# A fused attention, Fourier and MLP kernel on one core: weights fetched a step before they are converted, conversions tied to a place on VectorE, and a batch's products without padding

## Chip, cores and metric

One core of a Trainium2 chip runs the whole program as one launch. The metric is the device time of an execution in microseconds, and the median over the runs stands for the kernel. TensorE is called PE, VectorE DVE, ScalarE ACT, GpSimd POOL, and SyncE, which issues most DMAs, SP.

## The reference

Three layers follow one another. B=2, H=8, S=768, D=48, so the model width is 384. `w_ch1` and `w_ch2`, `w_in` and `w_out` arrive as float64, `w_sg` as float32.

```python
def _attn_ref(r, k, v, w, u):
    for t in range(S):
        kt, vt, rt, wt = (k[:, :, t], v[:, :, t], r[:, :, t], w[:, :, t])
        cur = np.einsum('bhd,bhe->bhde', u[None] * kt, vt)
        y[:, :, t] = np.einsum('bhd,bhde->bhe', rt, state + cur)
        state = wt[:, :, :, None] * state + np.einsum('bhd,bhe->bhde', kt, vt)

def _moe_ref(x, w_ch1, w_ch2):
    mixed = np.real(np.fft.fft(np.fft.fft(x, axis=1), axis=2)).astype(np.float32)
    u = x + mixed
    un = (u - mean(u)) / np.sqrt(var(u) + 1e-06)
    return u + np.maximum(un @ w_ch1, 0.0) @ w_ch2

def _moe2_ref(x, w_in, g_ln, w_sg, b_sg, w_out):
    u, v = split(gelu(x @ w_in))
    v_n = (v - mean(v)) / np.sqrt(var(v) + 1e-06) * g_ln
    v_s = np.einsum('ts,bsd->btd', w_sg, v_n) + b_sg[None, :, None]
    return x + (u * v_s) @ w_out
```

## The kernel before

**Attention.** Eight pairs of heads, n = 0 to 7; batch 0 has n = 0 to 3, batch 1 the others. A pair's 768 tokens are six chunks of 128. `prep` (L185) loads decays, r, k and v and scales them on DVE. `own_term` (L266) makes the term of u: six products dg_ps of the elementwise r·k with two columns of u, then dv on DVE. `scores` (L289) makes the products sc_ps of r and k in a chunk and masks them on DVE. `chunk_states` (L304) turns k with the identity (kn_ps), multiplies it with v (kv_ps) and runs the state through the chunks with a scan on DVE (U, L321). `values` (L326) adds what the state gives (L333) and what the chunk itself gives (L336) in y_ps. `radix6` (L340) starts the Fourier transform. Products in float32 take two instructions on PE. The products dg_ps, kn_ps, kv_ps and those of L336 are written 128 columns wide, though 2, 112, 96 and 96 of the columns are used; what lies past them is overwritten by the next product or not read.

**Fourier and MLP.** `fourier` (L404) transposes, runs the radix-3 step on DVE (L427 to L430, tiles t, sc and Z) and multiplies with tables (x_ps, gh). `moe1` (L508 on) works on four halves, n = 0 to 3, of 384 tokens, and for each through 12 blocks f of w_ch1 and w_ch2: z_ps, then z_hi on ACT and z_lo on DVE (L557), then ch. Values are kept as a rounded part (hi) and a rest (lo), and a product is three: hi·hi, hi·lo, lo·hi. `gating` multiplies with w_in (win), mixes over the tokens (s_ps, wsg) and multiplies with w_out (wout).

**Weights.** `narrow` (L155) fetches a piece of float64 with a DMA on SP into a raw tile and makes float32 of its words with three operations on DVE: L162, L163 and L164. The first two write the tile st, of which there are two. `weights(f)` (L823) does this for w1 and w2 of a block; ACT then copies hi (L837) and writes its negative (L838), and an accumulating DMA on POOL adds the raw value (L842, or L840 for two blocks). Blocks 1 and 3 use the tiles us_hi and us_lo as raw space, blocks 0, 2, 10 and 11 share one tile w_raw, the others use places of later blocks' weights. So a fetch waits for the accumulating DMA of the block that had the space before. `load_split` and `load_all` (L167, L179) do the same for win (8 pieces), wsg (12, without conversion) and wout (4), with two raw tiles.

**What sets the order.** The Python code emits the work of attention, Fourier, MLP and weights by turns: `merge` draws steps of two generators, and `ahead(n)` (L876) emits `weights(f)` for all blocks below n, one from the ninth step of the attention on (WA, WB), the first four before the MLP, later LA = 6 blocks ahead of the MLP's step. A scheduler then puts the instructions of each engine in a queue by its own estimates; each engine runs its queue in order, and an instruction that waits holds up what stands behind it. `after` (L151) ties later fetches to the last y of attention so far.

```python
        nc.vector.tensor_scalar(out=st, in0=top, scalar1=3, scalar2=0x3FFFFFF8, op0=ALU.logical_shift_left, op1=ALU.bitwise_and)
        nc.vector.scalar_tensor_tensor(out=st, in0=top, scalar=0xC0000000, in1=st, op0=ALU.bitwise_and, op1=ALU.bitwise_or)
        nc.vector.scalar_tensor_tensor(out=x, in0=low, scalar=29, in1=st, op0=ALU.logical_shift_right, op1=ALU.bitwise_or)
```

## Time and profile before

| | us |
|---|---|
| Median of three runs | 450.96 (449.62 to 455.56) |
| Profiled execution, its own time | 449.04 |
| Its span, first to last instruction | 447.3 |
| PE busy | 419.6 |
| DVE busy | 271.7 |
| ACT busy | 160.2 |
| POOL busy | 100.3 |

Times in the rows below count from the span's start. In an order of time, a row is start, duration in us, engine, line, operation, the tile written and those read, shape and count; what stands in brackets is how long the engine stood still before it, and what ended that. PE's mean granted clock over the span was 0.966 of full speed.

### The profile page before, as it was taken

The numbers are of one execution on the slowest core, as the hardware profiler recorded it, in microseconds if no ns is written. First come the engines' busy times: TensorE is split into PE (matmuls) and PEld (weight loads), VectorE is DVE, ScalarE is ACT, GpSimd is POOL, SyncE is SP. The second block draws the span as 40 slices with busy tenths as digits, with TensorE's granted clock in tenths as the row PEclk, the third lists the DMA queues.
The fourth block names the chain that finished last, engine by engine and source line by source line (L and its number), as shares of the span: only waits on it lengthen the run. The fifth ranks groups of instructions, "written<-read, shape, count | busy, mean of one in ns | idle before, by whom it ended". The sixth has DMA issues, their size and how long they took to land.

```text
span 447.3 us, 6662 instructions
## 1 busy us (share of the span) xinstructions
PE 419.6 (94%) x2502; PEld 398.2 (89%) x2502; DVE 271.7 (61%) x543; ACT 160.2 (36%) x365; POOL 100.3 (22%) x127
## 2 busy tenths in 40 slices
PE   9879959999899997999978999999989999999994
PEld 8769958897699996999968999999889998999994
DVE  5996869988589686656676316311488437502322
ACT  3432513732547265434234215313554214131100
POOL 2001210022313241311242002003455424001230
PEclk9657997999999999999999999999999999999998
DMA  7956793231276762203330000002432000200002
GB/s 247 318 131 164 233 271 77 36 116 27 98 264 113 190 106 74 34 1 91 120 90 18 2 0 1 0 1 70 125 88 72 0 3 1 88 19 0 1 21 95
DMA packets 17642, 38.09 MB, mean 85 GB/s; under 512 B 2304, under 2 KB 9344, under 8 KB 17472
## 3 DMA queue, kind: packets, MB, share of 16 engines
q1 hardware_dynamic: 14160, 31.66, 22.7%
q0 software_dynamic: 3440, 5.90, 7.3%
q8 instruction: 22, 0.36, 0.3%
q14 instruction: 20, 0.16, 0.1%
HBM read 28.70 MB, written 2.36 MB: 69 GB/s over the span
## 4 chain that ended last, share of the span: by engine, by line
PE 52%; DVE 16%; DMA 14%; issue 9%; ACT 4%; POOL 3%; SPq 1%; POOLq 0%; DVEq 0%; ACTq 0%
PE s_ps L112 11%; PE o_ps L112 6%; PE z_ps L112 6%; PE ch L112 5%; PE u_ps L112 5%; PE x_ps L115 4%; DMA w_raw<-in_w 3%; DMA us_hi<-in_w 3%; PE y_ps L336 3%; PE v_ps L112 3%; PE gh L115 2%; DMA raw<-in_win 2%; DMA raw<-in_wsg 2%; DMA w<-w_raw 2%; PE sc_ps L297 2%
## 5 line engine op out<-in xcount | busy, mean ns | idle before, releaser
L112 PE MATMUL z_ps<-us_hi,w 128*128 128x384 f32 x288 | 79.3, 340 | 2.6 <-ACT us_hi L532 2.1
L112 PE MATMUL ch<-z_hi,w 128*128 128x384 f32 x288 | 80.4, 339 | 0.5 <-ACT z_hi L556 0.5
L557 DVE SCALAR_TENSOR_TENSOR z_lo<-z_ps,z_hi 128x384 fp32r<-128x384 f32 x48 | 26.6, 553 | 60.5 <-ACT z_hi L556 60.5
L112 PEld LDWEIGHTS z_ps<-us_hi,w 128*128 128x128 f32 x288 | 52.5, 188 | 4.1 <-ACT us_hi L532 2.7
L112 PEld LDWEIGHTS ch<-z_hi,w 128*128 128x128 f32 x288 | 52.3, 188 | 1.8 <-ACT z_hi L556 1.1
L112 PE MATMUL ch<-z_lo,w 128*128 128x384 f32 x144 | 49.4, 343 | 3.4 <-DVE z_lo L557 3.2
L112 PE MATMUL z_ps<-us_lo,w 128*128 128x384 f32 x144 | 48.4, 336 | 0.0
L556 ACT ACTIVATE z_hi<-z_ps 128x384 fp32r<-128x384 f32 x48 | 23.5, 490 | 57.7 <-PE z_ps L112 38.5
L642 DVE SCALAR_TENSOR_TENSOR t_g<-s_ps,g,bsg 128x384 f32<-128x384 f32 x16 | 9.5, 615 | 41.8 <-PE s_ps L112 41.8
L112 PE MATMUL s_ps<-wsg_hi,vn_hi 128*128 128x384 f32 x96 | 32.5, 339 | 0.0
L112 PE MATMUL s_ps<-wsg_lo,vn_hi 128*128 128x384 f32 x96 | 32.5, 339 | 0.0
L112 PE MATMUL s_ps<-wsg_hi,vn_lo 128*128 128x384 f32 x96 | 32.5, 339 | 0.0
L112 PEld LDWEIGHTS ch<-z_lo,w 128*128 128x128 f32 x144 | 27.0, 188 | 5.2 <-DVE z_lo L557 5.2
L646 POOL TENSOR_TENSOR vn_lo<-t_g,vn_hi 128x384 fp32r<-128x384 f32 x16 | 16.4, 1033 | 55.7 <-ACT vn_hi L645 55.7
L112 PEld LDWEIGHTS z_ps<-us_lo,w 128*128 128x128 f32 x144 | 27.1, 188 | 0.1
L842 POOL DMA_DIRECT2D w<-w_raw x10 | 12.2, 1220 | 64.9 <-DVE Xh L254 31.6
L336 PE MATMUL y_ps<-v,sc 128*128 128x128 f32 x144 | 24.7, 294 | 0.0
L336 PEld LDWEIGHTS y_ps<-v,sc 128*128 128x128 f32 x144 | 23.3, 213 | 0.1
L645 ACT CAST vn_hi<-t_g 128x384 fp32r<-128x384 f32 x16 | 8.0, 513 | 37.9 <-DVE t_g L643 27.9
L177 POOL TENSOR_TENSOR wsg_lo<-raw,wsg_hi 128x384 fp32r<-128x384 f32 x12 | 12.4, 1036 | 32.3 <-ACT wsg_hi L176 32.2
L115 PE MATMUL x_ps<-dft,Z 128*128 128x256 f32 x72 | 16.9, 380 | 2.7 <-DVE Z L430 2.7
L509 POOL TENSOR_TENSOR z_lo<-uc,z_hi 128x384 fp32r<-128x384 f32 x7 | 7.1, 1010 | 50.4 <-ACT z_hi L508 50.4
(232 smaller groups left out, 963.7 us busy)
## 6 DMA issues: line engine op xcount, KB each, us to landing
w_raw<-in_w SPq DMA_DIRECT2D x20, 384.0 KB, 5.3
w<-w_raw POOLq DMA_DIRECT2D x10, 384.0 KB, 4.5
rk<-in_rk SPq DMA_DIRECT2D x4, 768.0 KB, 6.3
raw<-in_win SPq DMA_DIRECT2D x8, 384.0 KB, 3.3
v<-in_v SPq DMA_DIRECT2D x6, 384.0 KB, 5.9
raw<-in_wsg SPq DMA_DIRECT2D x12, 192.0 KB, 2.4
out<-o SPq DMA_DIRECT2D x12, 192.0 KB, 2.0
P<-in_wx SPq DMA_DIRECT2D x4, 387.0 KB, 4.8
```

The source lines that it names most:

```text
L112: nc.tensor.matmul(o, lhsT=x, rhs=y, start=start and i == 0, stop=stop and i == len(ps) - 1)
L115: nc.tensor.matmul(o, lhsT=a, rhs=b, start=start, stop=stop)
L177: nc.gpsimd.tensor_tensor(out=w.lo[:, to], in0=x, in1=w.hi[:, to].bitcast(F32), op=ALU.subtract)
L297: nc.tensor.matmul(sc_pss[h][:, i, :], lhsT=kt[hs, c * C:(c + 1) * C], rhs=rt[hs, c, :], start=True, stop=True)
L336: nc.tensor.matmul(y_ps[:, at:at + C], lhsT=sc[h][:, i, :], rhs=v[:, c], start=c == h == 0, stop=True, skip_group_check=True)
L509: nc.gpsimd.tensor_tensor(out=parts.lo, in0=x, in1=parts.hi.bitcast(F32), op=ALU.subtract)
L556: nc.scalar.activation(out=z.hi, in_=z_ps, func=AF.Relu)
L557: nc.vector.scalar_tensor_tensor(out=z.lo, in0=z_ps, scalar=0.0, in1=z.hi.bitcast(F32), op0=ALU.max, op1=ALU.subtract)
L642: nc.vector.scalar_tensor_tensor(out=t, in0=s_ps[h], scalar=g[:, f:f + 1], in1=bsg[:, hs], op0=ALU.mult, op1=ALU.add)
L645: nc.scalar.copy(vn.hi[:, f, 3 * h:3 * h + 3], th)
L646: nc.gpsimd.tensor_tensor(out=vn.lo[:, f, 3 * h:3 * h + 3], in0=th, in1=vn.hi[:, f, 3 * h:3 * h + 3].bitcast(F32), op=ALU.subtract)
L842: nc.gpsimd.dma_start(out=t[:, 1].bitcast(F32), in_=raw.bitcast(F32)[:, :, :NST], accum_op=ALU.add)
```

## The change

`narrow` is split: `fetch` issues the DMA and `narrow` only converts. `weights(f)` now only fetches and returns its tiles; `convert` does the rest, and `ahead` calls it for a block once the next one has been fetched (LAG = 1; LA goes from 6 to 7). `load_all` fetches piece o + 1 before it converts piece o. The first operation of every conversion is tied with `keep_in_program_order`: the scheduler may not put it ahead of the DVE operation that the program emitted just before it. In batch 1 dg_ps, kn_ps, kv_ps and the products of L336 are written 2, 112, 96 and 96 columns wide; batch 0 keeps 128.

```diff
@@ -26,7 +26,8 @@
 WA = 8
 WB = 3
 KC = 9
-LA = 6
+LA = 7
+LAG = 1
 RG = [[3,3,3,3],[0,0,0,0]]
 KV = range(8)
 NJ = 0
@@ -152,33 +153,44 @@
         if gate is not None:
             tc.add_manual_dep(getattr(ins, "ins", ins), getattr(gate, "ins", gate).name, mybir.DependencyInfo(mybir.DependencyClass.Sync, mybir.DependencyReason.DATA), reason="later weights")
 
-    def narrow(raw, src, o):
-
+    def fetch(raw, src, o):
         after(nc.sync.dma_start(out=raw, in_=src[:, o:o + NST]))
+
+    def narrow(raw):
         st = stage.tile([C, NST], U32, name="st", tag="st", bufs=2)
         word = raw.bitcast(U32).rearrange("p (n two) -> p n two", two=2)
         low, top = word[:, :, 0], word[:, :, 1]
         x = raw.bitcast(U32)[:, :NST]
-        nc.vector.tensor_scalar(out=st, in0=top, scalar1=3, scalar2=0x3FFFFFF8, op0=ALU.logical_shift_left, op1=ALU.bitwise_and)
+        first = nc.vector.tensor_scalar(out=st, in0=top, scalar1=3, scalar2=0x3FFFFFF8, op0=ALU.logical_shift_left, op1=ALU.bitwise_and)
+        if True:
+            tc.keep_in_program_order(first)
         nc.vector.scalar_tensor_tensor(out=st, in0=top, scalar=0xC0000000, in1=st, op0=ALU.bitwise_and, op1=ALU.bitwise_or)
         nc.vector.scalar_tensor_tensor(out=x, in0=low, scalar=29, in1=st, op0=ALU.logical_shift_right, op1=ALU.bitwise_or)
         return x.bitcast(F32)
 
-    def load_split(w, src, o, at):
-
-        to = slice(at, at + NST)
+    def load_piece(src, o):
+
         raw = raws[0].tile([C, NST], I64, name="raw", tag="raw", bufs=2)
         if src.dtype == I64:
-            x = narrow(raw, src, o)
-        else:
-            x = raw.bitcast(F32)[:, :NST]
-            nc.sync.dma_start(out=x, in_=src[:, o:o + NST])
+            fetch(raw, src, o)
+            return o, raw, None
+        x = raw.bitcast(F32)[:, :NST]
+        nc.sync.dma_start(out=x, in_=src[:, o:o + NST])
+        return o, raw, x
+
+    def split_piece(w, o, raw, x):
+        to = slice(o, o + NST)
+        if x is None:
+            x = narrow(raw)
         nc.scalar.copy(w.hi[:, to], x)
         nc.gpsimd.tensor_tensor(out=w.lo[:, to], in0=x, in1=w.hi[:, to].bitcast(F32), op=ALU.subtract)
 
     def load_all(w, src, n):
+        got = load_piece(src, 0)
         for o in range(0, n, NST):
-            load_split(w, src, o, o)
+            later_on = load_piece(src, o + NST) if o + NST < n else None
+            split_piece(w, *got)
+            got = later_on
             yield
 
 
@@ -277,7 +289,8 @@
         dg_ps = ps(b, [C, 512], "dg_ps", DB)
         for c in range(NC_):
 
-            nc.tensor.matmul(dg_ps[:, 2 * c:2 * c + C], lhsT=prod[:PR, c], rhs=uh[:, None, 2 * p:2 * p + 2].to_broadcast([PR, C // 2, 2]), start=True, stop=True)
+            k = C // 2 if b == 0 else 1
+            nc.tensor.matmul(dg_ps[:, 2 * c:2 * c + 2 * k], lhsT=prod[:PR, c], rhs=uh[:, None, 2 * p:2 * p + 2].to_broadcast([PR, k, 2]), start=True, stop=True)
         nc.vector.tensor_tensor(out=dv.rearrange("p c (h e) -> p c h e", h=2), in0=v[:, :, :2 * D].rearrange("p c (h e) -> p c h e", h=2),
                                 in1=dg_ps[:, :2 * NC_].rearrange("p (c h o) -> p c h o", h=2, o=1).to_broadcast([C, NC_, 2, D]), op=ALU.mult)
         return dv
@@ -304,15 +317,17 @@
     def chunk_states(ap, b, ends, kt, v, U):
 
         kn = ap([C, NC_ - 1, PR], "kn")
+        w = C if b == 0 else PR
         for g0, g1 in ((0, 3), (3, 5)):
             kn_ps = ps(b, [C, 3, C], "kn_ps", KB)
             for c in range(g0, g1):
-                nc.tensor.matmul(kn_ps[:, c - g0], lhsT=kt[:, c * C:(c + 1) * C], rhs=ident[:PR], start=True, stop=True)
+                nc.tensor.matmul(kn_ps[:, c - g0, :w], lhsT=kt[:, c * C:(c + 1) * C], rhs=ident[:PR, :w], start=True, stop=True)
             nc.scalar.copy(kn[:, g0:g1], kn_ps[:, 0:g1 - g0, :PR])
         kv_all = ps(b, [PR, 512], "kv_ps", VB)
         kv_ps = kv_all[:, :(NC_ - 1) * 2 * D].rearrange("p (c e) -> p c e", c=NC_ - 1)
         for c in range(NC_ - 1):
-            nc.tensor.matmul(kv_all[:, c * 2 * D:c * 2 * D + C], lhsT=kn[:, c], rhs=v[:, c], start=c == 0, stop=True, skip_group_check=c > 0)
+            e = C if b == 0 else 2 * D
+            nc.tensor.matmul(kv_all[:, c * 2 * D:c * 2 * D + e], lhsT=kn[:, c], rhs=v[:, c, :e], start=c == 0, stop=True, skip_group_check=c > 0)
         kvs = f_room([PR, 2 * D, NC_ - 1], "kvs") if b == 0 else ap([PR, 2 * D, NC_ - 1], "kn")
         for c in range(NC_ - 1):
             nc.scalar.activation(out=kvs[:, :, c], in_=kv_ps[:, c], func=AF.Copy, scale=ends[:PR, c:c + 1])
@@ -333,7 +348,8 @@
                 nc.tensor.matmul(y3[:, i, 0:3:2], lhsT=rt[:, c, :], rhs=U[:, :, c - 1], start=i == 0, stop=True, skip_group_check=True)
             for h in range(2):
                 at = (3 * i + h) * D
-                nc.tensor.matmul(y_ps[:, at:at + C], lhsT=sc[h][:, i, :], rhs=v[:, c], start=c == h == 0, stop=True, skip_group_check=True)
+                e = C if b == 0 else 2 * D
+                nc.tensor.matmul(y_ps[:, at:at + e], lhsT=sc[h][:, i, :], rhs=v[:, c, :e], start=c == h == 0, stop=True, skip_group_check=True)
         return nc.vector.tensor_tensor(out=yo.rearrange("p i (h e) -> p i h e", h=2), in0=y3[:, :, 0:3:2], in1=dv[:, c0:c0 + 3].rearrange("p i (h e) -> p i h e", h=2), op=ALU.add)
 
     def radix6(x, y, Z, es, G):
@@ -763,7 +779,7 @@
                 for i in range(2):
                     weight_pool(i, inner)
                 for f in range(NF1):
-                    weights(f)
+                    convert(*weights(f))
                 m1 = inner.enter_context(tc.tile_pool(name="m1", bufs=1))
                 run(moe1(m1, HALVES, uT, w1, w2))
             with tc.tile_pool(name="x2p", bufs=1) as pool:
@@ -831,8 +847,14 @@
         else:
             raw = wpool[0].tile([C, 2, NST], I64, name="w_raw", tag="w_raw")
         t = wpool[f >= NW].tile([C, 2, 2, DM], F32R, name=f"w_{f}", tag=f"w_{f}")
-        for i, (w, nm) in enumerate(((w1, "w1"), (w2, "w2"))):
-            x = narrow(raw[:, i] if raw is not None else us[i], ins[nm], f * DM)
+        places = us if raw is None else (raw[:, 0], raw[:, 1])
+        for place, nm in zip(places, ("w1", "w2")):
+            fetch(place, ins[nm], f * DM)
+        return f, t, raw, places
+
+    def convert(f, t, raw, places):
+        for i, w in enumerate((w1, w2)):
+            x = narrow(places[i])
             w[f] = Split(t[:, 0, i], t[:, 1, i])
             nc.scalar.copy(t[:, 0, i], x)
             nc.scalar.mul(t[:, 1, i], t[:, 0, i].bitcast(F32), -1.0)
@@ -871,13 +893,17 @@
                            a_room([C, 6 * DM], "Z").rearrange("p (z e) -> p z e", z=6))
             return made[b]
 
-        done = 0
-
-        def ahead(n):
+        done, fetched = 0, []
+
+        def ahead(n, most):
             nonlocal done
-            for f in range(done, min(n, NF1)):
-                weights(f)
-            done = max(done, min(n, NF1))
+            while done < min(n, most):
+                fetched.append(weights(done))
+                done += 1
+                while fetched and fetched[0][0] < done - LAG:
+                    convert(*fetched.pop(0))
+            while fetched and fetched[0][0] < n - LAG:
+                convert(*fetched.pop(0))
 
         m1 = low.enter_context(tc.tile_pool(name="m1", bufs=1, side="right"))
         early[0] = m1
@@ -891,7 +917,7 @@
                 if got == 0:
                     break
                 if n >= WA:
-                    ahead(min(GF, 1 + (n - WA) // WB))
+                    ahead(1 + (n - WA) // WB, GF)
             dump("y0", made[0][0])
             four = fourier(0, f_room, *made[0], uT[0])
             merge(islice(four, 4), att_steps, F0, False, LEAD)
@@ -914,10 +940,10 @@
                     dump("u0", uT[0])
                     late.close()
                     weight_pool(1, late, side="right")
-                ahead(min(12 * n + k + 1 + LA, NF1 if n or k >= E0 else NW))
+                ahead(12 * n + k + 1 + LA, NF1 if n or k >= E0 else NW)
                 yield
 
-        ahead(GF)
+        ahead(GF + LAG, GF)
         mixing = moe1(m1, HALVES, uT, w1, w2)
         merge(first(), second(), FR)
         att.close()
```

Three places in DVE's queue. The first is pair 3 of the attention: U_102 is its state scan, y_693 and prod belong to the next pair's `prep`, ab and Z to `radix6` of the pair before. Before:

```order
L347 TENSOR_TENSOR ab<-ab 128x2x96
L349 TENSOR_TENSOR Z<-ab 128x2x96
L162 TENSOR_SCALAR st<-us_hi 128x384
L253 SCALAR_TENSOR_TENSOR y_693,unit<-P,y_693 128x768
L348 SCALAR_TENSOR_TENSOR Z<-ab 128x2x96
L350 TENSOR_TENSOR Z<-ab 128x2x96
L321 SCALAR_TENSOR_TENSOR U_102<-dec,kvs 48x240 x2
L163 SCALAR_TENSOR_TENSOR st<-us_hi,st 128x384
L300 TENSOR_TENSOR sc<-sc_ps,later 128x384
L337 TENSOR_TENSOR y_116<-y_ps,dv 128x3x96
L300 TENSOR_TENSOR sc<-sc_ps,later 128x384
```

and now:

```order
L363 TENSOR_TENSOR ab<-ab 128x2x96
L365 TENSOR_TENSOR Z<-ab 128x2x96
L167 SCALAR_TENSOR_TENSOR st<-us_lo,st 128x384
L265 SCALAR_TENSOR_TENSOR y_693,unit<-P,y_693 128x768
L336 SCALAR_TENSOR_TENSOR U_102<-dec,kvs 48x240
L364 SCALAR_TENSOR_TENSOR Z<-ab 128x2x96
L366 TENSOR_TENSOR Z<-ab 128x2x96
L336 SCALAR_TENSOR_TENSOR U_102<-dec,kvs 48x240
L313 TENSOR_TENSOR sc<-sc_ps,later 128x384
L353 TENSOR_TENSOR y_116<-y_ps,dv 128x3x96
L313 TENSOR_TENSOR sc<-sc_ps,later 128x384
L168 SCALAR_TENSOR_TENSOR us_lo<-us_lo,st 128x384
```

Before, the conversion of block 3 (us_hi) begins ahead of the scan. Now only the middle operation of block 1 (us_lo) stands there, whose first operation is some rows up. Block 0's conversion, which was spread over the rows of the kernel's start, now stands ahead of the scan of the pair before this one, and eight more conversion operations than before stand between this scan and the first radix-3 operations of batch 0.

The second is the radix-3 step of batch 1, three groups at a time, and the conversion of the last block (w_raw). Before:

```order
L557 SCALAR_TENSOR_TENSOR z_lo<-z_ps,z_hi 128x384
L348 SCALAR_TENSOR_TENSOR Z<-ab_904 128x2x96
L427 TENSOR_TENSOR sc<-Z 128x256 x3
L428 TENSOR_TENSOR Z<-Z 128x2x128 x3
L429 SCALAR_TENSOR_TENSOR Z<-sc,Z 128x2x128 x3
L162 TENSOR_SCALAR st<-w_raw 128x384
L430 TENSOR_TENSOR Z<-Z,sc 128x2x128 x3
L163 SCALAR_TENSOR_TENSOR st<-w_raw,st 128x384
L162 TENSOR_SCALAR st<-w_raw 128x384
```

and now:

```order
L573 SCALAR_TENSOR_TENSOR z_lo<-z_ps,z_hi 128x384
L364 SCALAR_TENSOR_TENSOR Z<-ab_904 128x2x96
L443 TENSOR_TENSOR sc<-Z 128x256 x3
L444 TENSOR_TENSOR Z<-Z 128x2x128 x3
L445 SCALAR_TENSOR_TENSOR Z<-sc,Z 128x2x128 x3
L446 TENSOR_TENSOR Z<-Z,sc 128x2x128 x3
L573 SCALAR_TENSOR_TENSOR z_lo<-z_ps,z_hi 128x384
L164 TENSOR_SCALAR st<-w_raw 128x384
L167 SCALAR_TENSOR_TENSOR st<-w_raw,st 128x384
L168 SCALAR_TENSOR_TENSOR w_raw<-w_raw,st 128x384
```

The conversion's first operation stood inside the radix-3 step; now the whole conversion comes behind it and behind a z_lo. On POOL the accumulating DMA of the block before it, f = 10, has moved from ahead of the last pair's three operations (L347, L349, L350) to behind them.

The third is the second half of the MLP, where win is converted (raw). Before, where half n = 1 ends and the next one starts (uc, us_lo):

```order
L557 SCALAR_TENSOR_TENSOR z_lo<-z_ps,z_hi 128x384
L162 TENSOR_SCALAR st<-raw 128x384
L163 SCALAR_TENSOR_TENSOR st<-raw,st 128x384
L164 SCALAR_TENSOR_TENSOR raw<-raw,st 128x384
L162 TENSOR_SCALAR st<-raw 128x384
L163 SCALAR_TENSOR_TENSOR st<-raw,st 128x384
L557 SCALAR_TENSOR_TENSOR z_lo<-z_ps,z_hi 128x384
L164 SCALAR_TENSOR_TENSOR raw<-raw,st 128x384
L526 SCALAR_TENSOR_TENSOR uc<-mu,uT_1578 128x384 x3
L557 SCALAR_TENSOR_TENSOR z_lo<-z_ps,z_hi 128x384
L533 TENSOR_TENSOR us_lo<-uc,us_hi 128x384 x3
```

and now, at the same place:

```order
L564 SCALAR_TENSOR_TENSOR rstd<-var,rstd 128x384
L573 SCALAR_TENSOR_TENSOR z_lo<-z_ps,z_hi 128x384 x8
L542 SCALAR_TENSOR_TENSOR uc<-mu,uT_1578 128x384 x3
L573 SCALAR_TENSOR_TENSOR z_lo<-z_ps,z_hi 128x384
L164 TENSOR_SCALAR st<-raw 128x384
L549 TENSOR_TENSOR us_lo<-uc,us_hi 128x384 x3
L167 SCALAR_TENSOR_TENSOR st<-raw,st 128x384
```

Before, the conversions of win alternate with z_lo from early in the half. Now eight z_lo stand there in a row, the first conversion starts at the half's end, and the others follow among the z_lo of the next two halves; those of wout have moved behind the first operations of the token mixing.

## Rows read from the trace of the kernel before

**Rows 1.** The page, busy time of each engine over the whole span.
```profile
PE 419.6 (94%) x2502; PEld 398.2 (89%) x2502; DVE 271.7 (61%) x543; ACT 160.2 (36%) x365; POOL 100.3 (22%) x127
```

**Rows 2.** Busy time by stretch, in us from the span's start; PEclk is TensorE's granted clock.
```profile
core 0: us, PE busy (x) PEld busy (x) DVE busy (x) ACT busy (x) POOL busy (x), PEclk, DMA share, GB/s
...
39.00:64.40 25.40, 23.45 (x199) 21.72 (x197) 19.94 (x45) 8.51 (x26) 3.64 (x4) 1.00 0.85 263
...
67.50:72.50 5.00, 5.00 (x24) 5.00 (x25) 5.00 (x11) 2.54 (x5) 0.00 (x0) 0.52 0.41 93
72.50:92.60 20.10, 19.68 (x166) 17.88 (x165) 19.65 (x46) 11.69 (x34) 1.74 (x2) 1.00 0.23 41
92.60:114.00 21.40, 19.29 (x118) 16.22 (x116) 18.50 (x38) 5.98 (x18) 6.72 (x8) 1.00 0.34 108
114.00:161.00 47.00, 46.55 (x299) 43.97 (x299) 35.99 (x81) 23.32 (x53) 11.11 (x12) 1.00 0.57 149
...
204.00:242.00 38.00, 34.38 (x190) 32.41 (x189) 28.19 (x57) 13.99 (x30) 11.87 (x11) 1.00 0.29 91
```

**Rows 3.** Order of time, PE: its stops, with what ended each.
```profile
67.50 0.74 PE L333 MATMUL y_ps<-U,Xl 112*128 112x96 f32 x2 [5.04 <-DVE U L321]
...
114.16 0.44 PE L112 MATMUL z_ps<-us_hi,w 128*128 128x384 f32 x1 [2.13 <-ACT us_hi L532]
...
161.20 0.61 PE L112 MATMUL z_ps<-us_hi,w 128*128 128x384 f32 x2 [0.48 <-DMA w<-w_raw]
...
172.41 0.89 PE L115 MATMUL x_ps<-dft,Z 128*128 128x256 f32 x3 [2.69 <-DVE Z L430]
...
225.80 0.44 PE L112 MATMUL ch<-z_lo,w 128*128 128x384 f32 x1 [1.06 <-DVE z_lo L557]
...
232.32 0.44 PE L112 MATMUL ch<-z_lo,w 128*128 128x384 f32 x1 [1.19 <-DVE z_lo L557]
...
240.71 0.44 PE L112 MATMUL ch<-z_lo,w 128*128 128x384 f32 x1 [0.94 <-DVE z_lo L557]
```

**Rows 4.** Order of time, DVE: first operations of conversions (L162), and a scan.
```profile
47.15 0.36 DVE L162 TENSOR_SCALAR st<-us_hi 128x384 uint32<-128x384 uint32 x1 [1.85 <-DMA us_hi<-in_w]
...
64.44 0.36 DVE L162 TENSOR_SCALAR st<-us_hi 128x384 uint32<-128x384 uint32 x1 [3.46 <-DMA us_hi<-in_w]
...
66.14 1.31 DVE L321 TENSOR_TENSOR_SCAN U<-dec,kvs 48x240 f32<-48x240 f32 x2
...
171.29 0.64 DVE L162 TENSOR_SCALAR st<-w_raw 128x384 uint32<-128x384 uint32 x1 [1.35 <-DMA w_raw<-in_w]
```

**Rows 5.** Chain that ended last, at the weights of block f=8: start, us, what.
```profile
146.69 5.07 DMA w_raw<-in_w
...
156.75 4.41 DMA w<-w_raw
```

**Rows 6.** Order of time, PE: padded products at full clock, and a narrow one.
```profile
46.09 1.16 PE L280 MATMUL dg_ps<-uh,prod 112*128 112x128 f32 x8
47.09 1.25 PE L315 MATMUL kv_ps<-W,kn 128*112 128x128 f32 x10
48.18 0.51 PE L333 MATMUL y_ps<-U,rk 112*128 112x96 f32 x2
48.51 0.63 PE L336 MATMUL y_ps<-v,sc 128*128 128x128 f32 x4
48.97 0.51 PE L333 MATMUL y_ps<-U,rk 112*128 112x96 f32 x2
...
349.91 0.28 PE L701 MATMUL n_ps<-fine,ones 128*128 128x6 f32 x2
350.05 0.48 PE L112 MATMUL v_ps<-win_hi,x_hi 128*128 128x512 f32 x1
```

**Rows 7.** Order of time, DVE: conversion operations one after the other.
```profile
139.99 0.35 DVE L162 TENSOR_SCALAR st<-w_raw 128x384 uint32<-128x384 uint32 x1
140.26 0.54 DVE L164 SCALAR_TENSOR_TENSOR w_raw<-w_raw,st 128x384 uint32<-128x384 uint32 x1
140.73 0.55 DVE L163 SCALAR_TENSOR_TENSOR st<-w_raw,st 128x384 uint32<-128x384 uint32 x1
```

## Prediction

> **What bounds the kernel now.** I read the page's busy line first: TensorE (PE) is busy 419.6 of 447.3 us, 94%, VectorE (DVE) 271.7 [rows 1]. So a time saved elsewhere counts only where PE stands still, and a time saved on PE counts only where nothing else stands behind it. Next, the busy time by stretch [rows 2]. From 39 to 64.4 PE has 23.45 of 25.4 us, from 92.6 to 114 19.29 of 21.4, from 114 to 161 46.55 of 47: PE-bound. From 67.5 to 92.6 DVE is busy 5.00 of 5.00 and 19.65 of 20.1 us: there DVE decides, and PE, also busy, is close behind. From 204 to 242 both have air (PE 34.38, DVE 28.19 of 38).
>
> Then PE's order of time, for the stops and who ended them [rows 3]: 5.04 us before y_ps at 67.50 (the state scan U, L321), 2.13 before the first z_ps at 114.16 (us_hi on ACT), 0.48 at 161.20 (weights of a block), 2.69 before x_ps at 172.41 (Z, L430) and 1.06, 1.19 and 0.94 at 225.80, 232.32 and 240.71 (z_lo, L557). The change can reach all but the second. DVE's order of time says why U was late: ahead of it stands the first conversion operation of a block (L162, us_hi), which waited 3.46 us for its DMA at 64.44, and before that another one 1.85 us at 47.15; at 171.29 a third one, which sits between two of the four operations of the Z group, waited 1.35 us [rows 4]. A queue in order lets a wait for weights, which nobody needs yet, hold up a scan that PE needs at once.
>
> **Prices.** One conversion is three operations; their starts lie 0.27 and 0.47 us apart [rows 7], so a TENSOR_SCALAR and two STT cost 0.27+0.47+0.47 = 1.21 us of DVE, a block (w1 and w2) 2.42. For the padded products, full clock [rows 6]: dg (47.09-46.09)/8 = 0.125 us a row, kv (48.18-47.09)/10 = 0.109, y (48.97-48.51)/4 = 0.115; a product is two rows. A narrow product is not in the trace of these lines; the nearest is n_ps, 6 columns, at (350.05-349.91)/2 = 0.070. So a row of 128 columns can fall to 0.070 at most, not to nothing. For 96 of 128 columns (kv, y) I scale by columns: 0.109 to 0.082 and 0.115 to 0.086; kn, which has no row of its own here, as kv, 112 of 128, -0.014. For dg I take 0.080, near n_ps: -0.045. Batch 1 has 48 rows of dg, 40 of kn, 40 of kv and 96 of y: 2.2 + 0.6 + 1.1 + 2.8 = 6.7 us of PE. The ends are 0 (something other than columns sets a row) and, with every one of these rows at 0.070, 48 x 0.055 + 80 x 0.039 + 96 x 0.045 = 10.1.
>
> **Stretch 39 to 92.6.** Fetching a step ahead takes us_hi's wait away from before U: the operation that heads a conversion is now pinned behind whatever the program emitted last, and in the new order the block converted ahead of U (pair 3) is one whose fetch started long before. But f=0's conversion, which sat in the start, now lies where DVE had the wait at 47.15: 2.42 us more, and between U and the radix-3 operations there are 13 conversion operations where there were 5: 8 x 0.39 = 3.15 us. DVE's idle time here is 1.85 + 3.46 us; less 2.42 that leaves 2.9, plus the two operations (2 x 0.27) that no longer stand around pair 1's scan in the start, half of which PE passes on: 3.2 at the most. U itself comes 3 to 5 us earlier and PE's 5.04 shrinks to 2 or less; but what is late next is x_ps at 92.6, which waits for a DVE that has been full since 67.5. There is also a new wait: SP fetches f=2 into w_raw only when f=0's accumulating DMA is through, so not before 54 us (47.15 + 2.42 and 4.41 [rows 5]), and its conversion stands on DVE right behind U, with prod, rk and dv of the next pair queued behind it. If it lands as late as the us_hi of before (64.44), with U then at 63, it costs up to 1.5 us. Between 0 and -3.2 I take -1.6, the middle, since that DVE is full is measured and the new wait is not.
>
> **92.6 to 114**, PE-bound: of the products without padding dg 12, y 20, kv 10, kn 10 rows: 0.54 + 0.58 + 0.27 + 0.14 = -1.5. (In 67.5 to 92.6 dg 12, y 28, kv 20 and kn 20 rows, 2.2 us by the same prices, are hidden beneath DVE; 12 more of dg lie before.) Sum -3.1 at the first z_ps; the 2.13 us there remain, they are a chain through PE, DVE and ACT.
>
> **114 to 161**, PE-bound and behind it the weights: dg 12, kn 10, kv 10, y 48 rows, 2.3 us, of which at most 0.48 + 1.8 can show, since the weights of block f=8 end only at 161.16: fetch 5.07 us after a buffer comes free, conversion, accumulating DMA 4.41 [rows 5]. Between the fetch's landing (151.76) and that DMA (156.75) lie 5 us for 2.42 of conversion; the chain is moved by the -3.1 and by a conversion in one piece, which I put at 1 to 1.5 us less. I take -1.4; ends 0 and -2.3. Sum -4.5.
>
> **161 to 182.** The Z group is now ahead of the last block's conversion on DVE, so the 1.35 us wait and the 0.64 us operation leave the gap of 2.69 at 172.41. What is late next: this block's weights, needed at 182. They wait for the accumulating DMA of f=10, which now stands behind three operations of POOL that belong to the last pair (ab, Z, Z). So not 2.69 but half of it, -1.3 (0 to -2.7). Sum -5.8.
>
> **204 to 242.** The conversions of win, whose fetches DVE waits for between two z_lo, go to the boundary after it. Gaps of 1.06 + 1.19 + 0.94 = 3.19 disappear; PE then runs 34.38 us of work of which nothing else is late. I take -3.0 (0 to -3.2). The conversions land where PE is saturated later on and DVE has room; at the next boundaries three more operations (1.2 us) stand among z_lo and ch, which I put at 0 (up to +1). Wsg and wout are needed late, 0.
>
> **Sum:** -1.6 - 1.5 - 1.4 - 1.3 - 3.0 = -8.8 us. The profiled execution took 449.04; 440.2 in its frame. The median of the runs is 450.96, 1.9 above: 442.1, said as 442.
>
> **Rivals.**
> *The weight load sets a narrow row.* Each of these rows loads 128 (kv 112) columns of weights. If that takes as long as a row now does, the unpadding is worth nothing in time: -1.5 falls away, and most of -1.4, leaving -1.6 - 0.5 - 1.3 - 3.0 = -6.4, or 444.5. For it: dg, kv and y cost nearly the same now, whatever their operands. Against it: n_ps at 0.070, with 128 columns of weights [rows 6]. The Trainium skill, TensorE: Matmul & The Clock Gate, section LDWEIGHTS (loading the stationary operand), says that a load takes its columns divided by 1.2, in ns, so by an estimate from that page 107 ns for 128: the unpadding would then give under 2 us. n_ps here, two rows in 0.14 us, does not agree with it. 0.10.
>
> *The moves do nothing on balance.* DVE is full where its wait was taken away, the new fetch of f=2 is as late as the old one of f=3, the last block is held by POOL, and only PE-bound products and half the win gaps show: -1.5 - 0.5 - 1.5 = -3.5, 447.5. For it: 19.65 of 20.1 us on DVE [rows 2]. Against: PE's gaps have single, named causes [rows 3, 4]. 0.14.
>
> *The clock falls: slower.* After the 5.04 us stop the granted clock is 0.52, 1.2 GHz, from 67.5 to 72.5 and then 1.00, 2.4 GHz [rows 2, 3]. The 2.13 us stop before 114.16 left it at 1.00 in 114 to 161. In 67.5 to 92.6 PE gets 2.2 us less to do and DVE 3.15 more: PE waits more often, in pieces. If these let the clock fall at 72.5 and stay down until 92.6, its 19.68 busy us there take twice as long: +19.7 - 8.8 = +10.9, 462. It decides if pieces come near the 5.04 stop; what I expect is 5 us spread over 20, in pieces far below it, and the largest stop itself gets smaller. The Trainium skill, same page, section HAM oscillation — how this bites in real kernels, describes a kernel that starts each of its tiles cold since it waits before each; the first stop here behaves so, no other does. 0.08.
>
> *More than forecast.* The stop at 67.5 vanishes, the clock stays at 1.00, f=2 comes in time, and narrow rows fall to 0.070, so that 92.6 to 114 gives 12 x 0.055 + 20 x 0.039 + 20 x 0.045 = 2.3: -3.2 - 2.3 - 2.3 - 2.7 - 3.2 = -13.7, 437.3. 0.10.
>
> **Chances.** The forecast has 0.58, with a range of its own of 438.5 to 446. About 2% (9 us, below 441.9) is what a measurement of this kernel can tell from no change, and the forecast lies on that line: 0.30 of its 0.58 below. With 0.10 of the last case and a little of the others: faster 0.42, within 0.49, slower 0.09. The range reaches from 435 to 451: all but the clock and the ends of the others.
>
> **What would show it.** Right: y_ps of pair 3 near 63 to 65 with a gap under 3; x_ps of the first transform at 90 to 92; batch 1's dg rows at about 0.08, y at 0.086; first z_ps near 111; x_ps without a gap at 167 to 169; no z_lo gaps between 200 and 240. Wrong: a wait of DVE for w_raw after pair 3's scan that takes the 3 us back, dg rows still at 0.11 to 0.125, a granted clock near 0.5 after 72, or a stop of PE of more than 2 us for the weights of f=8 or f=11.

## The result and the profile after

The changed kernel takes 446.9 us (442.76 to 449.82, 18 runs), the kernel before 450.87 (449.1 to 455.56, 18 runs); the ratio is 0.9906, with a 95% interval from 0.9883 to 0.9928. It is faster by 4 us, where 8.8 were forecast. The ratios leave out runs more than 1.5% above the fastest of their kernel: here the one of 449.82 us, and 446.08 in the run with blocks 2 and 3 later, whose median is 439.16 without it. Its profiled execution took 446.3 us with a span of 444.6, 2.7 less than before. The page's first line, which answers [rows 1], says that PE is as busy as before:

```profile
PE 419.5 (94%) x2502; PEld 399.3 (90%) x2502; DVE 270.9 (61%) x543; ACT 161.1 (36%) x365; POOL 99.8 (22%) x127
```

419.5 us against 419.6: PE's busy time has not fallen. How much of that is the columns, and how much a granted clock that was low for longer (below), this line doesn't tell. PE's stops in order of time answer [rows 3]; the number in brackets is how long PE stood still, and what ended it:

```profile
63.38 0.59 PE L348 MATMUL y_ps<-U,Xl 112*128 112x96 f32 x2 [1.04 <-DVE U L336]
...
78.65 0.74 PE L348 MATMUL y_ps<-U,rk 112*128 112x96 f32 x2 [0.95 <-DVE U L336]
...
82.73 1.65 PE L310 MATMUL sc_ps<-rk 48*128 48x128 f32 x12 [1.20 <-DVE rk L266]
...
113.55 0.44 PE L113 MATMUL z_ps<-us_hi,w 128*128 128x384 f32 x1 [2.11 <-ACT us_hi L548]
...
160.03 0.59 PE L113 MATMUL z_ps<-us_hi,w 128*128 128x384 f32 x2 [0.17 <-DMA w<-w_raw]
...
181.34 0.62 PE L113 MATMUL z_ps<-us_hi,w 128*128 128x384 f32 x2 [1.13 <-DMA w<-w_raw]
...
233.06 0.41 PE L113 MATMUL ch<-z_hi,w 128*128 128x384 f32 x1 [0.87 <-DVE uT L583]
233.91 0.90 PE L113 MATMUL ch<-z_hi,w 128*128 128x384 f32 x2 [0.43 <-DVE uT L583]
...
275.18 1.28 PE L113 MATMUL ch<-z_hi,w 128*128 128x384 f32 x3 [0.87 <-DVE uT L583]
```

The stop of 5.04 us before pair 3's y_ps is down to 1.04, 4.1 us earlier; x_ps no longer stops at all, and none of the three stops before z_lo is left. In their place there are three stops before ch that DVE's uT ends (L583), two of some 1 us between 78 and 83, and 1.13 for the weights of the last block. The same places of PE's order in both traces show where time was won and lost (us from the span's start; the last column is the change over the stretch that ends there):

| place in PE's order | before | after | stretch |
|---|---|---|---|
| first y_ps that needs a state | 25.07 | 25.25 | +0.18 |
| y_ps of pair 3 (U) | 67.50 | 63.38 | -4.30 |
| first x_ps, batch 0 | 92.56 | 91.61 | +3.17 |
| first z_ps | 114.16 | 113.55 | +0.34 |
| z_ps with the weights of f=8 | 161.20 | 160.03 | -0.56 |
| var, half n=1 | 197.33 | 194.39 | -1.77 |
| mu, end of half n=1 | 226.95 | 222.31 | -1.70 |
| var, half n=2 | 243.42 | 239.11 | +0.33 |
| var, half n=3 | 282.26 | 279.22 | +1.27 |
| last product | 441.36 | 438.31 | -0.01 |

So 4.3 us were won at the scan, and 3.2 of them lost again within 28 us; 1.7 were won where win's conversions had stood, and 1.6 lost at the two ends of halves after it. Of these 1.6, 1.5 belong to this one execution: the changed kernel was profiled a second time, as the last of the runs below, and there var and mu of n=1 and var of n=2 and n=3 lie at 194.59, 222.50, 237.77 and 277.88, so that the first end gives -1.20 and the second +1.27. The first loss is seen in busy time by stretch, which answers [rows 2]; PEclk is the granted clock:

```profile
72.00:76.00 4.00, 4.00 (x34) 3.66 (x33) 4.00 (x10) 3.51 (x12) 0.00 (x0) 1.00 0.29 91
76.00:80.00 4.00, 3.05 (x21) 2.81 (x22) 3.96 (x10) 2.80 (x11) 0.00 (x0) 0.83 0.00 0
80.00:84.00 4.00, 2.80 (x20) 2.56 (x19) 4.00 (x10) 1.26 (x2) 0.00 (x0) 0.50 0.10 12
84.00:88.00 4.00, 4.00 (x22) 3.78 (x21) 4.00 (x12) 3.05 (x7) 2.07 (x2) 0.50 0.38 61
88.00:92.00 4.00, 4.00 (x32) 3.76 (x32) 3.23 (x10) 2.40 (x8) 0.87 (x2) 0.89 1.05 163
```

DVE is full from 72 to 88, and from 76 to 84 PE, which waits for it, is busy 5.85 of 8 us; from about 79 on the clock is 0.50, 1.2 GHz, for some 10 us. The kernel before had such a stretch too, after its long stop [rows 2, 67.5 to 72.5]; here it lies later, where PE has the products of two pairs to do before x_ps.

The second loss is seen on DVE where half n=1 ends:

```profile
227.85 0.35 DVE L164 TENSOR_SCALAR st<-raw 128x384 uint32<-128x384 uint32 x1
...
229.52 0.55 DVE L167 SCALAR_TENSOR_TENSOR st<-raw,st 128x384 uint32<-128x384 uint32 x1
229.99 1.48 DVE L582 TENSOR_TENSOR ch<-ch,rstd 128x384 f32<-128x384 f32 x3
231.39 1.06 DVE L168 SCALAR_TENSOR_TENSOR raw<-raw,st 128x384 uint32<-128x384 uint32 x1
232.38 0.54 DVE L583 TENSOR_TENSOR uT<-uT,ch 128x384 f32<-128x384 f32 x1
```

Ahead of the operations that bring the old half's ch to uT (L582, L583) and among them stand the three of one conversion (L164, L167, L168), the last of which took 1.06 us where [rows 7] has 0.54. PE has three banks for ch and can't start the new half's before uT has read the old one. What comes behind differs between the two profiles. Busy time from 234 to 238, in the changed kernel's first profile and in its second:

```profile
234.00:238.00 4.00, 3.95 (x14) 3.44 (x15) 3.12 (x7) 1.37 (x3) 1.11 (x2) 0.70 0.34 98
234.00:238.00 4.00, 3.85 (x19) 3.34 (x20) 3.31 (x8) 1.49 (x3) 1.40 (x2) 1.00 0.36 98
```

The stops for uT before this stretch are the same in both (0.87 and 0.43 us), and the clock fell in one of them only; that is the 1.5 us. Last, the unpadded rows, to be set beside [rows 6]:

```profile
75.57 1.43 PE L293 MATMUL dg_ps<-uh,prod 112*128 112x2 f32 x12
76.85 0.85 PE L430 MATMUL t_ps<-ident,yr 128*128 128x128 f32 x6
...
107.71 0.60 PE L352 MATMUL y_ps<-v,sc 128*128 128x96 f32 x4
108.15 0.52 PE L348 MATMUL y_ps<-U,rk 112*128 112x96 f32 x2
```

Twelve rows of dg with 2 columns take 1.28 us, 0.107 each, and four of y with 96 columns 0.44, 0.110, where 0.080 and 0.086 were forecast and [rows 6] have 0.125 and 0.115.

### The profile page after: what moved, and what is told of

It is laid out like the page before. It is cut to its first block, busy times and chain, and to the rows that moved or that the text cites. A ratio compares the mean times of both kernels' runs of the same rounds, so it can differ in the third digit from the quotient of the medians.

```text
span 444.6 us, 6645 instructions
## 1 busy us (share of the span) xinstructions
PE 419.5 (94%) x2502; PEld 399.3 (90%) x2502; DVE 270.9 (61%) x543; ACT 161.1 (36%) x365; POOL 99.8 (22%) x127
## 4 chain that ended last, share of the span: by engine, by line
PE 56%; DVE 16%; DMA 12%; issue 8%; ACT 3%; POOL 2%; SPq 1%; POOLq 0%; DVEq 0%; ACTq 0%
PE s_ps L113 11%; PE z_ps L113 10%; PE ch L113 9%; PE o_ps L113 6%; DMA w<-w_raw 5%; PE u_ps L113 5%; DMA w_raw<-in_w 3%; PE v_ps L113 3%; PE x_ps L116 2%; PE gh L116 2%; DMA raw<-in_wsg 2%; DVE st L167 2%; PE sc_ps L310 2%; DVE sc L313 2%; DVE w_raw L168 1%
## 5 line engine op out<-in xcount | busy, mean ns | idle before, releaser
L113 PE MATMUL ch<-z_hi,w 128*128 128x384 f32 x288 | 82.6, 345 | 2.2 <-DVE uT L583 2.2
L113 PEld LDWEIGHTS ch<-z_hi,w 128*128 128x128 f32 x288 | 53.5, 191 | 4.5 <-ACT z_hi L572 2.3
L352 PE MATMUL y_ps<-v,sc 128*128 128x96 f32 (+1 forms) x144 | 24.2, 294 | 0.0
L348 PE MATMUL y_ps<-U,rk 112*128 112x96 f32 x50 | 13.7, 365 | 7.1 <-DVE U L336 7.1
```

What stands on the lines that cost most here:

```text
L113: nc.tensor.matmul(o, lhsT=x, rhs=y, start=start and i == 0, stop=stop and i == len(ps) - 1)
L348: nc.tensor.matmul(y3[:, i, 0:3:2], lhsT=rt[:, c, :], rhs=U[:, :, c - 1], start=i == 0, stop=True, skip_group_check=True)
L352: nc.tensor.matmul(y_ps[:, at:at + e], lhsT=sc[h][:, i, :], rhs=v[:, c, :e], start=c == h == 0, stop=True, skip_group_check=True)
```

## The experiments

Eleven kernels ran, the changed one again among them. Ratios are to the kernel before, on the same chip.

**Padding again.** Do the columns matter?

```diff
-            k = C // 2 if b == 0 else 1
+            k = C // 2
-        w = C if b == 0 else PR
+        w = C
-            e = C if b == 0 else 2 * D
+            e = C
```

> The changed kernel with batch 1 padded to 128 columns again; the fetches ahead and the pins stay. If columns set a row's time (the forecast's prices), PE has 6.7 us more to do and the time goes up by 3 to 5 us, to 450 to 452, so that nothing of the gain is left; dg rows come at 0.12 and kv, y at 0.109 and 0.115 against 0.08, 0.08 and 0.086. If something other than columns sets a row (the rival), the rows of the changed kernel are those its trace shows, dg 0.107, y 0.1075, kv 0.08 to 0.10, the padding costs 48 x 0.012 + 96 x 0.0075 + 40 x 0.009 = 1.7 us of PE and at most 1.2 us of time: 447 to 448.1.

446.19 us (444.52 to 447.18), ratio 0.9871 (0.9834 to 0.9908). Putting the padding back costs no time that these runs can tell: the intervals of the two overlap, and this one's median is the lower. The price by columns, which gave 450 to 452, falls. But equal time need not mean equal work. In the profiles it takes from pair 3's U to var of n=1 133.84 us here and 131.01 in the changed kernel (131.25 in its second profile); and the mean granted clock over the runs is 0.975 here and 0.963 there. In the two other pairs of kernels below that differ by the padding alone the padded one has the higher clock too, 0.970 against 0.967 and 0.979 against 0.976. That the clock takes back what the narrower products give would fit, but it is not shown.

**What sets a row.** The disputed cost by itself:

```diff
+        for M, W in ((128, 128), (128, 96), (128, 64), (128, 2), (64, 128), (64, 64), (64, 2), (32, 2)):
+            tp = cps.tile([C, 512], F32, name=f"t{M}x{W}", tag="c")
+            for i in range(16):
+                nc.tensor.matmul(tp[:M, :W], lhsT=(ident, ones)[i % 2][:, :M], rhs=ident[:, :W], start=True, stop=True)
```

> The changed kernel with eight blocks of 16 float32 products (32 rows each) at its end, whose results nobody reads: weights of 128 columns with products of 128, 96, 64 and 2 columns, weights of 64 columns with 128, 64 and 2, and weights of 32 columns with 2. If the columns of the product set a row, 128, 96, 64 and 2 columns come at about 0.11, 0.085, 0.07 and under 0.07, whatever the weights. If the columns of the weights set a row, the first four come all at 0.10 to 0.11, and the blocks with weights of 64 and 32 columns and 2 columns of product at some 0.05 and 0.03.

PE's order of time at the end of this kernel; each line is the two rows of one product, "128*64 128x2" is 128x64 of weights and a product 2 columns wide, and the next start is the next line's:

```profile
440.21 0.39 PE L978 MATMUL t128x<-ident 128*128 128x128 f32 x2
440.43 0.39 PE L978 MATMUL t128x<-ident,ones 128*128 128x128 f32 x2
...
443.31 0.39 PE L978 MATMUL t128x<-ident 128*128 128x96 f32 x2
443.53 0.39 PE L978 MATMUL t128x<-ident,ones 128*128 128x96 f32 x2
...
450.40 0.36 PE L978 MATMUL t128x<-ident 128*128 128x2 f32 x2
450.62 0.36 PE L978 MATMUL t128x<-ident,ones 128*128 128x2 f32 x2
...
452.20 0.57 PE L978 MATMUL t128x<-ident 128*128 128x2 f32 x2
452.63 0.57 PE L978 MATMUL t128x<-ident,ones 128*128 128x2 f32 x2
...
464.11 0.26 PE L978 MATMUL t64x<-ident 128*64 128x2 f32 x2
464.23 0.26 PE L978 MATMUL t64x<-ident,ones 128*64 128x2 f32 x2
...
466.09 0.20 PE L978 MATMUL t32x<-ident 128*32 128x2 f32 x2
466.15 0.20 PE L978 MATMUL t32x<-ident,ones 128*32 128x2 f32 x2
```

With 128 columns of weights a row takes 0.11 us, whether the product has 128, 96 or 2 columns. With 64 and 2 it takes 0.06, with 32 and 2 0.03; with 64 and a product of 128 it is 0.11 again (461.60 to 461.82 for two rows). So the larger of the two counts of columns sets a row. In this kernel batch 1's weights keep their 128 or 112 columns, so the unpadding could save only the little by which a row stood above that: dg 0.119 to 0.110 over 12 rows in the same place of both traces (131.79 before, 131.18 after). The Trainium skill, TensorE: Matmul & The Clock Gate, section LDWEIGHTS (loading the stationary operand), gives the columns of the weights divided by 1.2 as a load's ns, by an estimate from it 107, 53 and 27 for 128, 64 and 32 columns. The 0.11, 0.06 and 0.03 us of the narrow products here lie a little above that.

The fourth pair of lines is a surprise: the same rows take 0.21 us there. Busy time by stretch:

```profile
447.50:451.00 3.50, 3.50 (x34) 3.50 (x33) 0.00 (x0) 0.00 (x0) 0.00 (x0) 1.00 0.00 0
...
454.00:457.50 3.50, 3.50 (x18) 3.48 (x18) 0.00 (x0) 0.00 (x0) 0.00 (x0) 0.50 0.00 0
```

PE was busy without a break, and its clock fell from 1.00 to 0.50 near 451, behind the products of 64 columns and the first few of 2. More on it below.

**Without the pins.** Is it the pin or the fetch ahead that moves the conversions?

```diff
-        if True:
-            tc.keep_in_program_order(first)
```

> The changed kernel without the pins: fetches a step ahead and the unpadded products stay, and the scheduler may put a conversion's first operation anywhere. If the pins carry the gain (the moves of win and of the last block's conversion on DVE), the win gaps of some 3 us come back, but then the boundary's conversions may leave, so the time is 447 to 450; if the fetch ahead carries it, the time is as the changed kernel's, 446 to 447.5.

453.46 us (449.44 to 454.83), ratio 1.0035 (1.0006 to 1.0064): all of the gain is gone, more than either theory said. PE's stops are those of the kernel before:

```profile
66.92 0.74 PE L346 MATMUL y_ps<-U,Xl 112*128 112x96 f32 x2 [4.19 <-DVE U L334]
...
225.69 0.44 PE L113 MATMUL ch<-z_lo,w 128*128 128x384 f32 x1 [1.08 <-DVE z_lo L571]
...
232.22 0.44 PE L113 MATMUL ch<-z_lo,w 128*128 128x384 f32 x1 [1.19 <-DVE z_lo L571]
```

**The pins alone**, in the kernel before, with fetch and conversion in one step and the padding:

```diff
+        first = nc.vector.tensor_scalar(out=st, in0=top, scalar1=3, scalar2=0x3FFFFFF8, op0=ALU.logical_shift_left, op1=ALU.bitwise_and)
+        tc.keep_in_program_order(first)
```

> The kernel before with the pins alone: no fetch ahead, no unpadding. If the pins alone carry the gain, the time is 446 to 448, as the changed kernel's. If the pins need the fetch ahead (a pinned operation waits for its own fetch, issued in the same step), DVE stands in conversions for DMAs of 5 to 8 us, and the time is 450 or more.

448.19 us (444.11 to 449.44), ratio 0.9918 (0.9884 to 0.9953). The pins alone do what the whole change does, within the intervals. DVE's longest wait for a fetch among the first four blocks is 1.22 us at 55.88: where the kernel before has 3.46 [rows 4]. Here a pinned operation waited for its own fetch no longer than the unpinned ones did.

**Win inside the halves.** Are the ends of halves what gives back the win gaps?

```diff
-            if k % 2 or n == 3:
+            if k % 2 and k != NF1 - 1 or n == 3 and k > 1:
```

> The changed kernel, in which the eight pieces of win are emitted at other steps of the MLP: at k = 1, 3, 5, 7, 9 of half n = 2 and from k = 2 on of n = 3, so that none is converted where one half ends and the next begins. If the three conversion operations that now stand among L542 to L583 at each of the two boundaries are what gives back the win gaps (DVE's chain there holds the three ch banks that PE needs), PE's stops before ch at 233.06, 233.91 and 275.18 fall to 0.3 or less and the time falls by 2 to 3 us against the changed kernel, to 444 to 445. If the boundaries stop PE anyway (add_ch alone, as the 0.23 us stop of the kernel before at 278.86), the time stays within 0.7 us of 446.9.

445.77 us (443.17 to 447.24), ratio 0.9864 (0.9824 to 0.9904). PE's stops:

```profile
233.36 0.79 PE L113 MATMUL ch<-z_hi,w 128*128 128x384 f32 x3 [0.23 <-ACT z_hi L572]
234.99 0.45 PE L113 MATMUL ch<-z_lo,w 128*128 128x384 f32 x1 [0.84 <-DVE z_lo L573]
...
273.14 0.79 PE L113 MATMUL ch<-z_hi,w 128*128 128x384 f32 x3 [0.23 <-ACT z_hi L572]
...
325.76 0.44 PE L113 MATMUL u_ps<-x_hi,win_hi 128*128 128x384 f32 x1 [1.76 <-ACT v L624]
...
328.35 0.45 PE L113 MATMUL u_ps<-x_hi,win_hi 128*128 128x384 f32 x1 [0.76 <-ACT v L624]
```

The stops for uT are gone. From mu to mu over the first end of a half it takes 39.78 us instead of 42.12, from mu to var over the second 13.53 instead of 14.79: 3.6 us together. The changed kernel's second profile, without the low clock at 234, has 40.59 and 14.79, so 1.5 of the 3.6 are the clock's and the conversions cost 0.81 + 1.26 = 2.1 us; for these the cause is shown. But 1.4 of them are lost again at u_ps, which now waits 1.76 and 0.76 us for v on ACT (L624), where the changed kernel waited 1.1 in all; and in the profiled run the first U came 0.54 us later. Median against median 1.1 us remain, less than the expected 2 to 3 and within the intervals.

**Less to convert.** What holds x_ps at 91.6, DVE's work or the clock? This kernel leaves out the second operation of the conversions of blocks 2 and 3.

```diff
+        if not short:
             nc.vector.scalar_tensor_tensor(out=st, in0=top, scalar=0xC0000000, ...
```

> The changed kernel without the second of the three conversion operations of blocks 2 and 3 (its weights come out without their sign and top exponent bits): four STT of 0.47 us, 1.9 us of DVE, less between pair 3's scan and the radix-3 step. If DVE's work sets x_ps there (it is busy in all but some 0.3 us from 64 to 90), x_ps comes 1.5 to 1.9 us earlier counted from the first U, 64.5 to 64.9 after it where it was 66.4, and the first z_ps follows by about 1. If what holds x_ps is the granted clock that fell to 0.50 from 79 to 89, it falls here too as long as PE still waits for DVE, and x_ps moves by less than 0.7.

From the first U to x_ps it takes 65.85 us, against 66.36 in the changed kernel (66.74 in its second profile): 0.5 to 0.9 less, not the 1.5 to 1.9 that DVE had less to do.

```profile
80.00:84.00 4.00, 2.60 (x14) 2.35 (x15) 4.00 (x12) 1.60 (x3) 0.34 (x1) 0.50 0.61 98
84.00:88.00 4.00, 4.00 (x26) 3.78 (x23) 4.00 (x13) 2.92 (x6) 1.39 (x2) 0.50 0.69 96
88.00:92.00 4.00, 4.00 (x26) 3.92 (x26) 0.92 (x3) 0.21 (x1) 0.00 (x0) 0.75 0.32 54
```

The clock fell here as well, and from 88 to 92 DVE had work for 0.92 us and PE for all four: at that place it is the slow PE that x_ps waits for. It ran once, so its 447.24 us are no comparison.

**Blocks 2 and 3 later.** The same question from the other side:

```diff
-                    ahead(1 + (n - WA) // WB, GF)
+                    ahead(1 + (n - WA) // WB, 2)
-            merge(islice(four, 4), att_steps, F0, False, LEAD)
+            def parts():
+                for i, got in enumerate(islice(four, 4)):
+                    if i == 1:
+                        ahead(GF + LAG, GF)
+                    yield got
+            merge(parts(), att_steps, F0, False, LEAD)
```

> The changed kernel, in which blocks 2 and 3 are emitted in the transform of batch 0 after its first x_ps, so that their conversions stand behind the first radix-3 operations and not between pair 3's scan and them. If DVE's conversions in 63 to 90 us hold x_ps, it comes 3 us or more earlier, at 88 to 89; DVE then does the same 4.8 us between 90 and 113, where it has 2.9 idle, so the first z_ps moves by -1 to +1. If the whole stretch to the first z_ps is bound by DVE's sum, the time stays within 1 us of 446.9; if only the place before x_ps is, it falls to 444 to 445.5.

440.86 us (438.39 to 446.08), ratio 0.972 (0.9658 to 0.9782): 6 us better than the changed kernel, more than either theory gave.

```profile
80.21 0.94 PE L310 MATMUL sc_ps<-rk 48*128 48x128 f32 x12 [0.37 <-DVE rk L266]
...
109.53 0.69 PE L113 MATMUL z_ps<-us_hi,w 128*128 128x384 f32 x1 [2.89 <-ACT us_hi L548]
```

```profile
64.00:68.00 4.00, 4.00 (x24) 4.00 (x22) 4.00 (x10) 1.95 (x3) 0.85 (x1) 0.57 0.15 45
...
80.00:84.00 4.00, 3.71 (x35) 3.42 (x36) 4.00 (x13) 2.56 (x4) 0.00 (x0) 1.00 0.36 52
84.00:88.00 4.00, 4.00 (x33) 3.68 (x32) 3.93 (x12) 2.23 (x8) 0.00 (x0) 1.00 0.27 66
...
108.00:114.00 6.00, 4.47 (x11) 3.67 (x12) 3.27 (x7) 3.91 (x9) 1.86 (x3) 0.57 0.26 101
```

With the twelve conversion operations of these blocks gone from 63 to 90, PE stops 0.37 us where it stopped 0.95 and 1.20, the clock, low for a short while after U, is 1.00 from 68 to 108, x_ps comes at 86.86 and the first z_ps at 109.53, 4 us earlier than in the changed kernel. Moving DVE's work to 90 to 113 cost less than it gave. (The blocks' fetches and ACT's copies moved with it.) In this profile the clock fell from 108 to 116 instead, and from the first z_ps to the first var it took 16.65 us, not 13.71. The six runs differ by the clock as well: means of 0.979 to 0.982 go with 438.4 to 439.2 us, 0.966 to 0.975 with 442.6 to 446.1.

**Both places**, and both with the padding, with the changed kernel on the same chip as a scale.

> The changed kernel with both moves: blocks 2 and 3 emitted after the first x_ps, win's pieces inside the halves. If the two places are separate causes, their gains add: 440.9 less 1 to 2.5, so 438.4 to 440, and the stops before ch at the two boundaries are 0.3 or less. If the gain at the boundaries is given back before u_ps as in the run with win alone (L624 on ACT), it stays at 440 to 441.

> The same with batch 1 padded to 128 columns. If unpadding saves what its rows show (1.2 to 1.7 us of PE, here in a stretch where PE and DVE are both full), this one is 1 to 1.7 us slower than the run before. If the narrow products cost a lower granted clock as often as they save, it is equal within 0.7 us, and its profile shows no stretch at 0.50 to 0.60 between 100 and 125.

> The changed kernel itself, on the same chip as the two others, as the scale for them: 446 to 447.5 if all is as said.

440.8 us (436.95 to 442.82), ratio 0.9775 (0.9731 to 0.982); 441.59 (438.24 to 443.84), 0.9794 (0.975 to 0.9838); 446.56 (442.77 to 448.71), 0.9897 (0.9855 to 0.9939). That the gains add is not seen: win inside is worth nothing measurable on top of the later blocks, though its stops are gone here too. With intervals of 2 to 3 us to either side, 1 us more could not be told. Taking the padding away is worth 0.8 us here with overlapping intervals, so again nothing that can be told from none, and neither profile has a low clock between 100 and 125. Win inside and padded without the later blocks, another run, says the same:

> The changed kernel with win's pieces inside the halves, as in the run before this one on win, and batch 1 padded to 128 columns. If the padding is worth nothing either way, the time is that of win inside alone, 445 to 446.5. If unpadding saves what the rows show before the first z_ps (1.2 us in the profiles), it is 446.5 to 447.2.

445.89 us (444.31 to 447.32), ratio 0.9875 (0.9832 to 0.9918), as with win inside alone. The version with blocks 2 and 3 later is the best found, with or without the rest.

## Why the prediction was wrong

The stops that it named were the right ones and went as it said: U came 4.1 us earlier (3 to 5 were forecast), PE's stop there is 1.04 (under 2), x_ps of batch 1 stops no more, the last block's weights are late next, and no z_lo gap is left between 200 and 240. What it took for their sizes and for what lies behind them failed in three steps. Nearest in number came a rival, the moves that do nothing on balance (447.5, at 0.14), and that was luck: its 0 for the stretch to 92.6 was -0.95, and its -1.5 for the products shows nowhere in the times of the padded runs.

**The price of a narrow row.** "For dg I take 0.080, near n_ps", and kv and y "by columns". The columns of the weights set these rows, and they didn't change. Measured in place, a row falls by some 0.009 (dg), 0.0075 (y) and 0.009 (kv): 48 x 0.009 + 96 x 0.0075 + 40 x 0.009 = 1.5 us of PE where 6.7 were forecast, and by the padded runs nothing of it shows in the time. n_ps, one product between two others, was no steady rate: 2 columns, product after product, take 0.11. The rival that named the weight load was right on the rows and had 0.10; its 444.5 missed too. The term of 92.6 to 114 was forecast at -1.5 and came out at +0.34, that of 114 to 161 at -1.4 and came out at -0.56. With the padding back the first of these stretches takes 22.38 us against 21.94, so the columns gave 0.4 there; why it is longer than the 21.60 of before stays open.

**The conversions at the ends of halves**, "which I put at 0 (up to +1)". They stand in the chain that empties ch for PE: 2.1 us at two ends by the run with win inside, and in the first profile 1.5 us of low clock behind the first of them. The term of -3.0 came out at -1.70 + 0.33 + 1.27 = -0.10 there and at -1.71 - 1.20 + 1.27 = -1.64 in the second profile.

**Stretch 39 to 92.6**, -1.6, came out at -0.95: near in size, not the whole reason. The new wait for f=2's fetch, feared at 1.5, was 0.34 us at 65.54. DVE was full, as said, but PE, which waits more often for a DVE with 13 conversion operations, lost its clock from 79 to 89. That is the rival for a slower kernel; it was worked out at 20 us of low clock and came with 10, at a place where the kernel before had lost its own 5 after 67.5. The prediction's sum counts neither the end of that first low stretch nor the new one, which has 0.08 as a rival. That rival also says that no other stop behaves like the one at 67.5; in the kernel before the clock is 0.50 from 25 to 35 as well, behind a stop of 3.30 us at 25.07. In the run with less to convert PE, not DVE, was last before x_ps. The run with blocks 2 and 3 later shows that 5 us of x_ps hang on where these conversions stand, and in all three kernels that have them later the clock is 1.00 from 72.5 to 92. How those 5 split between clock and DVE is not separated. (The prediction's 8 x 0.39 is 3.12 us, not 3.15; nothing hangs on it.)

**161 to 182** was forecast at -1.3, and by 197 had given -1.77, with the stop of 1.13 us for f=11 that the step named.

Of the change's three parts the pins carry the gain; neither the fetch ahead without them nor the unpadding gives any that these runs can tell. What the fetch ahead adds to the pins, with the padding in both, is 0.9918 to 0.9871, and these intervals overlap.

## What to carry to other kernels

Before a product is made narrower, look at what it loads: float32 rows with 128 columns of weights took 0.11 us here from 2 to 128 columns. Look at the granted clock before and after as well, and at a second profile before a loss is put down to the change. Work that nobody needs yet should stand in a queue behind what the next engine needs, and where it goes has to be priced too: look for the chain (a scan, a bank that must be emptied) which it will stand in. And count the conversions between two points of a full engine, not only the waits that leave it.

## What was not expected of the hardware

PE's granted clock fell from 1.00 to 0.50 (1.2 GHz) while PE was busy 3.50 of 3.50 us and never stopped; what it did before the fall were products of 64 and then 2 columns with 128 columns of weights. The Trainium skill, TensorE: Matmul & The Clock Gate, section HAM oscillation — how this bites in real kernels, tells of idle gaps; here there were none.

Where the clock is low differs between executions: from 234 to 238 in the first profile of the changed kernel and not in the second, and behind the first U until about 30 us in the profile with both places, until 36 to 39 in the others; pair 3's U came at 60.33 there, and at 63.2 to 64.4 in the other kernels with pins and fetch ahead. The changed kernel's spread (442.8 to 449.8 us) goes in part with its mean clock: 0.970 at 442.76 us, 0.960 at 449.82.

A SCALAR_TENSOR_TENSOR of DVE took 1.06 us instead of 0.55 at 231.39, and again at 273.51 (1.07). A TENSOR_TENSOR of POOL (uc, L553) ran beside it both times, from 231.02 and from 273.14 on; whether that is the cause was not tried.
